# Attention steps behind a gate taken in pairs, in a kernel of banded attention followed by a mixture of experts

## Chip, cores and metric

One core of a Trainium2 chip runs the whole program. The metric is the device time of one execution in microseconds (us). The kernel before took 825.73 to 827.17 us in three runs, 827.11 us in the median.

## What is computed

Eight heads of attention, four with a plain causal window of 32 positions and four with a window of 32 positions at a distance of 4, and then four experts on its output, each weighed by a probability:

```python
mask_plain = (rel >= 0) & (rel < window)                      # window 32
mask_dil = (rel >= 0) & (rel < window * dilation) & (rel % dilation == 0)
scores = np.where(masks, scale * np.matmul(q, k.transpose(0, 1, 3, 2)), -1e9)
attn = np.exp(scores - np.max(scores, axis=-1, keepdims=True))
attn = attn / (np.sum(attn, axis=-1, keepdims=True) + 1e-09)
x = np.matmul(attn, v)                # 4 x 8 x 576 x 64, then 2304 x 512
for e in range(E):                    # 4 experts, hidden size 1024
    h = np.maximum(x @ w1[e], 0.0)
    out += p[:, e:e + 1] * (h @ w2[e])
```

## The kernel before, in words

Every large product runs as three products of rounded halves (high by high, low by high, high by low), so each operand x, w1, w2 and h is split into a high half (ScalarE, L130 or L449) and a low half (VectorE or GpSimd, L127 and L455).

**The experts' stream** is a generator, `experts`, that hands out pieces. A visit is one quarter of one expert on 768 tokens, and has 13 pieces. `mm1_b` (L475 on) has five, each a product of six TensorE matmuls of 384 columns: S2 (then ScalarE copies the bank to u2, L482), S1 (copied to s5, L487), S3 (VectorE adds the bank to s5, L491), S4 (VectorE adds to u2, L496) and A22. A22 writes into the bank that L491 reads, so TensorE can't begin it before L491 is done. `mm1_a` has two such pieces for the next visit; after the second VectorE adds (L472), ScalarE makes a hidden half (L449) and VectorE the other (L455). `mm2` has six pieces in two lots of three; a piece is one tile of 128 tokens, six matmuls of 512 columns into one of two banks, and VectorE adds the bank to the sum (L544, named acc). A tile can begin only when the tile two before it has been added. The two lots stand on the two sides of `mm1_a`'s second piece. A piece says "room" after S2, S1 and `mm1_a`'s first, and "full" after S4 and A22. VectorE, ScalarE and GpSimd work through their instructions in the order in which the program writes them.

**Attention** has 24 steps of two groups each. A step is: 24 small matmuls for the scores (`s_qk`, tile sc, 48 records in the trace), six masked maxima on VectorE (`s_max`), a subtraction on GpSimd (`s_sub`), the exponential on ScalarE (`s_exp`), the sums and reciprocals on VectorE (`s_sum`, tiles su and rc), a multiplication on GpSimd (`s_norm`), three transposes on TensorE and one copy on ScalarE (`s_tr`, tiles pt and pts), and 24 small matmuls with v (`s_av`, tile po, 48 records) with two copies to x on ScalarE. The four banks of `pa` hold sc, pt and po in turn.

**The order.** A loop over rounds n writes, at the start of a round, the parts of attention that are due (the tables `first`, `apart`, `then`), and then takes pieces of the experts' stream, with one step of the queue of splits (`step`) after each. Steps 0 to 9 are needed before the gate OPEN, which lies at 56 us. The 14 steps behind it (10 to 23) follow table `then`: one step begins in each round of PACE = 10 pieces, and the parts of four steps that are under way stand together at the round's start: `s_sub`, `s_sum`, `s_tr`, `s_av`, `s_qk`, `s_norm`, `s_exp`, `s_max`. Splits of x for later tokens (`x_part`, on VectorE for odd parts, tiles xl) are taken at pieces that say "room"; differences of x (`x_sums`, L227) run on VectorE.

Of the kernel before, what the change touches and what calls it, by code (L numbers as in the profile page):

```python
# [48 lines left out]
def kernel(  # L49
# [194 lines left out]
    def attention(ap, xrp, pa):  # L244
# [125 lines left out]
        def s_av(n, gs):  # L370
# [3 lines left out]
            for i in range(GS):  # L374
                for half in range(2):
                    for k in range(len(gs)):
                        rows = slice(KB * k, KB * (k + 1))
                        for j in range(2):
                            c = i * 128 + 64 * (j ^ k) + QB * half
                            o = i * SB + QB * half  # L380
                            nc.tensor.matmul(  # L381
                                po[k][64 * j:64 * j + 64, o:o + QB],
                                v_s[rows, j, 2 * i + half, :], ts_[rows, c:c + QB],
                                start=True, stop=True,
                            )

            for k, (b, p, gi) in enumerate(gs):
                x = x_raw(b)[:, p, :]
                src = po[k][:, :GW]
                if p < NP // 2:  # L390
                    nt = GW // DILATION
                    dst = x.rearrange("q (r t) -> q r t", r=DILATION)
                    dst = dst[:, :, gi * nt:(gi + 1) * nt]
                    src = src.rearrange("q (t r) -> q r t", r=DILATION)
                else:
                    dst = x[:, gi * GW:(gi + 1) * GW]
                if 0 < n < 3:
                    nc.vector.tensor_copy(out=dst, in_=src)
                else:
                    nc.scalar.activation(out=dst, in_=src, func=AF.Copy)  # L400

        def load_masks():
# [21 lines left out]
        return chunk, load_masks, load_qk, load_v, stages  # L424
# [234 lines left out]
    with tc.manual_schedule():  # L659
# [14 lines left out]
        pools["chunk"], load_masks, load_qk, load_v, stages = attention(ap, xr_pool, pa)  # L674
# [16 lines left out]
        steps = [rest[i:i + 2] for i in range(0, len(rest), 2)]  # L691
# [17 lines left out]
        step_at = {at(n): n for n in range(len(steps))}  # L709
# [81 lines left out]
        for n, i, names in (  # L791
# [9 lines left out]
        qk_done = av_done = 0  # L801
# [6 lines left out]
        ready["qk"] = lambda m: m < qk_done + QKB and n >= waits.get(min(m, needed[1] + 2), 0)  # L808
        fenced = {2: (3, 0), 3: (3, 1), 4: (3, 1), 7: (START + 4, 0), 8: (START + 5, 0)}
        ready["v"] = lambda m: (  # L810
            m < av_done + VB
            and (m <= needed[1] or m <= qk_done and n >= OPEN)
# [37 lines left out]

        dummies(512, 512, 128)
        ffn = experts(begin)
        for n in range(at(len(steps) - 1) + 5):
# [12 lines left out]
            for k, order in enumerate((stages[early_order], stages[2])):  # L866
                for stage, after in order:
                    m = step_at.get(n - after, -1)
                    if m >= 0 and k == (m > needed[1]):
# [11 lines left out]
                        av_done += stage == s_av  # L881
# [3 lines left out]
            if n in step_at:  # L885
                qk_done += 1
            for i, names in when.get(n, ()):
                for name in names:
                    of = first_x if i < 2 else later
                    if name is None or name == "T2":  # L890
                        prepare(x_sums, i, of=of)
                    if name is not None:
                        prepare(x_part, i, name.upper(), of=of)
# [31 lines left out]
            for piece in range(PACE if n in step_at else 4):  # L925
                full = next(ffn)
                if n == OPEN and not piece:
                    s_max(step_at[n], steps[step_at[n]])
                step()
                if full != "full":  # L930
# [4 lines left out]
                    elif full == "room":  # L935
                        step(later)
        gate.add("over")
# [61 lines left out]
```

## Time and profile before

| | |
|---|---|
| median of three runs | 827.11 us (825.73 to 827.17) |
| profiled execution | 828.18 us, its span 826.4 us |
| TensorE (PE) busy | 817.3 us, 99% of the span |
| VectorE (DVE) busy | 488.2 us, 59% |
| GpSimd (POOL) busy | 387.5 us, 47% |
| ScalarE (ACT) busy | 316.3 us, 38% |
| granted clock of TensorE | 0.994 of full speed over the span |
| chain that ended last | PE 94%, DVE 3%, ACT 1%, DMA 1% |

A busy TensorE says little here, since the ends of matmuls are modelled and overlap: the time is read from the distance between the starts of matmuls that follow each other. In the stream a matmul of 512 columns starts 0.23 us after the one before and one of 384 columns 0.17 us after.

### The profile page before, as it was taken

To read this page: it belongs to the slowest core of one execution; us is meant where nothing else is said; L and a number is where in the kernel's file an instruction comes from. 1 tells how busy PE (TensorE), PEld (TensorE's weight loads), DVE (VectorE), ACT (ScalarE), POOL (GpSimd) and SP (SyncE) were. 2 spreads that over 40 slices of the span, in tenths; PEclk is the share of its full clock that TensorE was granted. 3 is DMA by queue.
4 is the path that set the end of the run, shared out by engine and by line. 5 is a ranking of instruction groups with operands and counts; after the bars stand their busy time and mean duration, and the time that the engine had idled before them with its cause. 6 is when DMAs were issued, how large, how long until landed. Compare 5 with 4: busy or idle time off the path is not lost.

```text
span 826.4 us, 15443 instructions
## 1 busy us (share of the span) xinstructions
PE 817.3 (99%) x6162; PEld 726.3 (88%) x6162; DVE 488.2 (59%) x1058; ACT 316.3 (38%) x749; POOL 387.5 (47%) x465
## 2 busy tenths in 40 slices
PE   8999999999999999999999999999999999999998
PEld 5878888889888888989989989989989989988987
DVE  5677666675666588554554554555555555555555
ACT  2445444455545455323323323323333333333321
POOL 4436877787767689343143143143143153153110
PEclk9899999999999999999999999999999999999999
DMA  7755433434321113110010010010010010010003
GB/s 231 227 147 147 148 113 92 141 107 127 104 90 52 52 69 129 59 52 25 26 52 27 26 52 26 26 52 26 27 51 26 26 52 26 27 51 1 1 26 127
DMA packets 46770, 59.15 MB, mean 72 GB/s; under 512 B 2905, under 2 KB 36313, under 8 KB 46699
## 3 DMA queue, kind: packets, MB, share of 16 engines
q1 hardware_dynamic: 46283, 57.75, 22.4%
q8 instruction: 48, 0.79, 0.4%
q10 hardware_dynamic: 416, 0.43, 0.1%
q14 instruction: 23, 0.19, 0.1%
HBM read 53.45 MB, written 4.72 MB: 70 GB/s over the span
## 4 chain that ended last, share of the span: by engine, by line
PE 94%; DVE 3%; ACT 1%; DMA 1%; issue 1%; POOL 0%; POOLq 0%; DVEq 0%; ACTq 0%
PE m L535 47%; PE m1y L431 24%; PE m1x L431 17%; PE po L381 2%; PE sc L300 1%; PE wt L775 1%; PE pt L361 1%; DMA r<-w 1%; DVE xr L227 1%; DVE acc L544 0%; ACT hh L449 0%; DVE s L491 0%; DVE sm L314 0%; DVE hl L455 0%; ACT xh_B L130 0%
## 5 line engine op out<-in xcount | busy, mean ns | idle before, releaser
L544 DVE SCALAR_TENSOR_TENSOR acc<-m,pn,acc 128x512 f32<-128x512 f32 (+1 forms) x271 | 202.3, 747 | 129.7 <-PE m L535 129.7
L535 PE MATMUL m<-w2h,hh 128*128 128x512 f32 x578 | 227.2, 393 | 0.0
L535 PE MATMUL m<-w2l,hh 128*128 128x512 f32 x578 | 225.5, 390 | 0.0
L127 POOL TENSOR_TENSOR g2l<-r,g2h 128x256 fp32r<-128x256 f32 x116 | 85.9, 768 | 234.4 <-PE m L535 212.8
L535 PE MATMUL m<-w2h,hl 128*128 128x512 f32 x578 | 178.8, 390 | 0.3 <-DVE hl L455 0.3
L449 ACT ACTIVATE hh<-s 128x384 fp32r<-128x384 f32 x92 | 48.4, 526 | 236.7 <-DVE s L472 187.4
L535 PEld LDWEIGHTS m<-w2h,hl 128*128 128x128 f32 x578 | 108.3, 188 | 24.3 <-DVE hl L455 0.8
L535 PEld LDWEIGHTS m<-w2h,hh 128*128 128x128 f32 x578 | 108.5, 188 | 21.4 <-DVE acc L544 1.5
L535 PEld LDWEIGHTS m<-w2l,hh 128*128 128x128 f32 x578 | 108.6, 188 | 19.6
L127 POOL TENSOR_TENSOR g1l<-r,g1h 128x256 fp32r<-128x256 f32 x93 | 69.1, 763 | 69.0 <-ACT g1h L130 69.0
L127 POOL TENSOR_TENSOR w2l<-r,w2h 128x512 fp32r<-128x512 f32 x58 | 74.8, 1307 | 46.8 <-ACT w2h L130 46.6
L491 DVE TENSOR_TENSOR s<-m1y,s 128x384 f32<-128x384 f32 x46 | 25.6, 557 | 96.0 <-PE m1y L431 92.9
L482 ACT ACTIVATE u<-m1y 128x384 f32<-128x384 f32 x46 | 22.6, 492 | 146.1 <-PE m1y L431 146.1
L455 DVE SCALAR_TENSOR_TENSOR hl<-s,hh 128x384 fp32r<-128x384 f32 x92 | 56.5, 614 | 27.4 <-ACT hh L449 27.2
L431 PE MATMUL m1y<-xh_T,g2h 128*128 128x384 f32 x152 | 51.4, 338 | 0.0
L431 PE MATMUL m1y<-xl_T,g2h 128*128 128x384 f32 x152 | 51.1, 336 | 0.0
L431 PE MATMUL m1y<-xh_T,g2l 128*128 128x384 f32 x152 | 51.0, 335 | 0.0
L130 ACT ACTIVATE g2h<-r 128x256 fp32r<-128x256 f32 x120 | 41.7, 405 | 0.4 <-POOL r L168 0.4
L431 PE MATMUL m1x<-xh_B,g2h 128*128 128x384 f32 x124 | 41.6, 336 | 0.2 <-ACT s L487 0.2
L431 PE MATMUL m1x<-xl_B,g2h 128*128 128x384 f32 x124 | 41.6, 336 | 0.0
L431 PE MATMUL m1x<-xh_B,g2l 128*128 128x384 f32 x124 | 41.4, 334 | 0.0
L130 ACT ACTIVATE w2h<-r 128x512 fp32r<-128x512 f32 x64 | 38.2, 622 | 1.3 <-DMA r<-w 1.3
(133 smaller groups left out, 1490.7 us busy)
## 6 DMA issues: line engine op xcount, KB each, us to landing
r<-w SPq DMA_DIRECT2D x63, 512.0 KB, 3.3
v_s<-vw SPq DMA_DIRECT2D x48, 192.0 KB, 4.5
k_s<-kT SPq DMA_DIRECT2D x23, 224.0 KB, 4.4
q_s<-qT SPq DMA_DIRECT2D x24, 192.0 KB, 4.5
out<-acc SPq DMA_DIRECT2D x17, 256.0 KB, 2.0
r<-w SPq DMA_DIRECT2D x2, 256.0 KB, 4.6
out<-acc SPq DMA_DIRECT2D x2, 128.0 KB, 2.0
k_s<-kT ACTq DMA_DIRECT2D x1, 224.0 KB, 3.3
```

Of the source, the lines that this page charges most:

```text
L127: lo_eng.tensor_tensor(out=lo, in0=src, in1=hi.bitcast(F32), op=ALU.subtract)
L130: nc.scalar.activation(out=hi, in_=src, func=AF.Copy)
L227: nc.vector.tensor_tensor(out=quarter(i, d), in0=quarter(i, a), in1=quarter(i, b), op=ALU.subtract)
L300: nc.tensor.matmul(banks[swap][o:o + QB, i * KB:(i + 1) * KB], q_s[h, c0:c0 + QB], k_s[h, c0:c0 + KB], start=True, stop=True, skip_group_c ...
L381: nc.tensor.matmul(po[k][64 * j:64 * j + 64, o:o + QB], v_s[rows, j, 2 * i + half, :], ts_[rows, c:c + QB], start=True, stop=True,)
L431: nc.tensor.matmul(bank, w[:, k], x[:, k], start=(first and k == 0 and i == 0), stop=(last and k == 1 and i == 2), skip_group_check=True,)
L449: nc.scalar.activation(out=hi, in_=src, func=AF.Relu)
L455: nc.vector.scalar_tensor_tensor(out=lo, in0=src, scalar=0.0, in1=hi.bitcast(F32), op0=ALU.max, op1=ALU.subtract)
L482: nc.scalar.activation(out=u2, in_=x, func=AF.Copy)
L491: nc.vector.tensor_tensor(out=s5, in0=x, in1=s5, op=ALU.add)
L535: nc.tensor.matmul(po, h, w[:, d], start=(n == 0 and x == 0), stop=(n == 3))
L544: nc.vector.scalar_tensor_tensor(out=acc[:, d], in0=po, scalar=pn[:, tt, e:e + 1], in1=acc[:, d], op0=ALU.mult, op1=ALU.add,)
```

## The change

Steps 11 to 23 are taken in pairs, step 10 and step 23 alone. Rounds behind the gate have 20 pieces where two steps begin (`PACE * len(new)`). Table `then` keeps only the start of step 10. A new generator, `pairs_of_steps`, writes the parts: the transposes of the old pair at the round's start; after the next piece both steps' po (`s_av` with `hold`) and the first step's copies to x; after the next the second step's copies; after the next the scores of the new pair and the first step's maxima; and then one link of the chain (max, sub, exp, sum, norm) after each piece, the second step one piece behind the first. Pieces that say "full" are passed over, and nothing is written after them. The last step's po comes after 141 pieces behind the gate, where it came after 152.

```diff
-        then = (
-            (s_sub, 1), (s_sum, 2), (s_tr, 3), (s_av, 4), (s_qk, 0), (s_norm, 2), (s_exp, 1),
-            (s_max, 0),
-        )
+        then = ((s_qk, 0), (s_max, 0))
...
+        def pairs_of_steps(new, old, begun, loaded):
+
+            for m in old:
+                s_tr(m, steps[m])
+            if old:
+                yield
+                for m in old:
+                    s_av(m, steps[m], True)
+                    if m == old[0]:
+                        s_out(m, steps[m])
+                yield
+                for m in old[1:]:
+                    s_out(m, steps[m])
+                loaded(0, len(old))
+                yield
+            if new and not begun:
+                for m in new:
+                    s_qk(m, steps[m])
+                s_max(new[0], steps[new[0]])
+                yield
+            chain = (s_max, s_sub, s_exp, s_sum, s_norm)
+            for i in range(1, len(chain) + len(new) - 1):
+                for k, m in enumerate(new):
+                    if i - k < len(chain):
+                        chain[i - k](m, steps[m])
+                if not begun and i == 2:
+                    loaded(len(new), 0)
+                yield
...
         def at(n):
 
+            back = max(0, n - needed[1])
+            n -= back - back // 2 - (back > 0)
             return n + sum(gap for gap, last in zip((GAP, GAP - 1), needed) if n > last)
...
-            return 3 if n <= needed[1] else 4
+            return 3 if n <= needed[1] else 1
...
-            for piece in range(PACE if n in step_at else 4):
+            new, old = ([m for m in late if at(m) == i] for i in (n, n - 1))
+            turns = turn(new, old, n == OPEN, loaded)
+            if n > OPEN:
+                next(turns)
+            for piece in range(PACE * len(new) or PACE):
                 full = next(ffn)
                 if n == OPEN and not piece:
                     s_max(step_at[n], steps[step_at[n]])
+                elif full != "full" or n == OPEN:
+                    next(turns, 0)
                 step()
```

In the rows of order, lines of the changed file are later by 32 in the experts' part (L535 is L567, L544 is L576, L491 is L523, L455 is L487, L431 is L463), and a number behind a name only tells one tile from the next.

TensorE, kernel before: the groups of one step (pt transposes, po, sc) stand in one row of groups between two tiles m.

```order
L535 MATMUL m_2020<-w2h,hl 128x512 x2
L361 MATMUL pt<-ident,sm 128x128 x3
L381 MATMUL po<-pts,v_s 64x32 x24
L300 MATMUL sc<-k_s,q_s 32x64 x24
L535 MATMUL m_2113<-w2h,hh 128x512
```

TensorE, changed kernel, the same place one round later: two steps' transposes, then a tile, then two steps' po, then a product m1y and a tile (left out here but for their ends), then two steps' scores.

```order
L567 MATMUL m_2120<-w2h,hl 128x512 x2
L361 MATMUL pt<-ident,sm 128x128 x6
L567 MATMUL m_2142<-w2h,hh 128x512
...
L567 MATMUL m_2142<-w2h,hl 128x512 x2
L381 MATMUL po<-pts,v_s 64x32 x48
L463 MATMUL m1y<-xh_B_0_498,g1h 128x384
...
L567 MATMUL m_2226<-w2h,hl 128x512 x2
L300 MATMUL sc<-k_s,q_s 32x64 x48
L567 MATMUL m_2296<-w2h,hh 128x512
```

The three groups of a step no longer touch each other, and each holds two steps.

VectorE, kernel before, the end of one step's part and the experts' work behind it: the maxima (L314, the last one shown) come right behind the sums, and then three tiles' additions, the add of `mm1_a` (L472), its low half (L455) and the next three additions follow with nothing between them.

```order
L314 ISA sm,nm<-sc,mask 128x64
L314 ISA nm 128x1
L544 SCALAR_TENSOR_TENSOR acc_725<-m_2337,pn,acc_725 128x512
L544 SCALAR_TENSOR_TENSOR acc_725<-m_2349,pn,acc_725 128x512
L544 SCALAR_TENSOR_TENSOR acc_725<-m_2359,pn,acc_725 128x512
L472 TENSOR_TENSOR s_2324<-m1y,s_2324 128x384
L455 SCALAR_TENSOR_TENSOR hl<-s_2324,hh 128x384
L544 SCALAR_TENSOR_TENSOR acc_725<-m_2387,pn,acc_725 128x512
L544 SCALAR_TENSOR_TENSOR acc_725<-m_2397,pn,acc_725 128x512
L544 SCALAR_TENSOR_TENSOR acc_725<-m_2407,pn,acc_725 128x512
```

VectorE, changed kernel, the same place in the round (17) of steps 13 and 14.

```order
L576 SCALAR_TENSOR_TENSOR acc_725<-m_1932,pn,acc_725 128x512
L576 SCALAR_TENSOR_TENSOR acc_725<-m_1958,pn,acc_725 128x512
L341 TENSOR_REDUCE su<-sm 128x6
L342 TENSOR_TENSOR su<-su,eps 128x6
L345 RECIPROCAL rc<-su 128x6
L504 TENSOR_TENSOR s_1838<-m1y,s_1838 128x384
L487 SCALAR_TENSOR_TENSOR hl<-s_1838,hh 128x384
L341 TENSOR_REDUCE su<-sm 128x6
L342 TENSOR_TENSOR su<-su,eps 128x6
L345 RECIPROCAL rc<-su 128x6
L576 SCALAR_TENSOR_TENSOR acc_725<-m_1998,pn,acc_725 128x512
L576 SCALAR_TENSOR_TENSOR acc_725<-m_2009,pn,acc_725 128x512
```

One step's sums now stand ahead of the add of `mm1_a`, the other's between its low half and the addition of tile m_1998, for which the tile after next, m_2019, waits.

VectorE, changed kernel, round 20 (steps 19 and 20), at `mm1_b`: between the maxima and the add of S3 (L523, s_3132), for which A22 waits, stand two splits of x and one step's sums, and the other step's sums come right behind.

```order
L314 ISA nm 128x1
L127 TENSOR_TENSOR xl_B_1_1908<-xr,xh_B_1_1907 128x2x192
L341 TENSOR_REDUCE su<-sm 128x6
L342 TENSOR_TENSOR su<-su,eps 128x6
L345 RECIPROCAL rc<-su 128x6
L127 TENSOR_TENSOR xl_B_1_2045<-xr,xh_B_1_2044 128x2x192
L523 TENSOR_TENSOR s_3132<-m1y,s_3132 128x384
L341 TENSOR_REDUCE su<-sm 128x6
```

In the kernel before a step's sums stand right ahead of its round's maxima, and the splits of x come behind these.

## Rows read from the trace of the kernel before

**Rows 1.** The page, part 1: busy us (share of the span) xinstructions by engine.

```profile
PE 817.3 (99%) x6162; PEld 726.3 (88%) x6162; DVE 488.2 (59%) x1058; ACT 316.3 (38%) x749; POOL 387.5 (47%) x465
```

**Rows 2.** Timeline, one step's groups: start us, busy us, engine, line, operation, tiles, count.

```profile
108.15 0.49 PE L361 MATMUL pt<-ident,sm 128*128 128x128 f32 x3
108.57 0.90 PE L381 MATMUL po<-pts,v_s 64*64 64x32 f32 x48
109.40 0.72 PE L300 MATMUL sc<-k_s,q_s 64*32 64x64 f32 x48
110.06 0.50 PE L535 MATMUL m<-w2h,hh 128*128 128x512 f32 x1
110.39 0.39 PE L535 MATMUL m<-w2l,hh 128*128 128x512 f32 x1
```

**Rows 3.** Timeline of TensorE around transposes alone (46.61), scores alone (68.84), po alone (268.44).

```profile
45.80 0.34 PE L431 MATMUL m1y<-xh_B,g1h 128*128 128x384 f32 x1
45.97 0.34 PE L431 MATMUL m1y<-xh_B,g1l 128*128 128x384 f32 x1
...
46.61 0.52 PE L361 MATMUL pt<-ident,sm 128*128 128x128 f32 x3
46.88 0.48 PE L535 MATMUL m<-w2h,hh 128*128 128x512 f32 x1
47.20 0.39 PE L535 MATMUL m<-w2l,hh 128*128 128x512 f32 x1
47.43 0.39 PE L535 MATMUL m<-w2h,hh 128*128 128x512 f32 x1
...
68.58 0.34 PE L431 MATMUL m1x<-xl_B,g1h 128*128 128x384 f32 x1
...
69.50 0.44 PE L431 MATMUL m1y<-xh_B,g1h 128*128 128x384 f32 x1
...
268.17 0.34 PE L431 MATMUL m1x<-xl_B,g1h 128*128 128x384 f32 x1
...
269.27 0.50 PE L535 MATMUL m<-w2h,hh 128*128 128x512 f32 x1
```

**Rows 4.** Tiles po and sc, one record's duration: ns min/median/max, first and last start.

```profile
L381 PE MATMUL po<-pts,v_s x1152: 211/219/313, 12.3 to 269.1; 64*64 64x32 f32 x192
L300 PE MATMUL sc<-k_s,q_s x1152: 212/216/241, 5.1 to 238.0; 64*32 64x64 f32 x192
```

**Rows 5.** Timeline, from the end of mm1_a's second piece to the third tile behind.

```profile
89.46 0.39 PE L535 MATMUL m<-w2h,hh 128*128 128x512 f32 x1
89.72 0.56 DVE L472 TENSOR_TENSOR s<-m1y,s 128x384 f32<-128x384 f32 x1 [0.39 <-PE m1y L431]
90.87 0.56 DVE L455 SCALAR_TENSOR_TENSOR hl<-s,hh 128x384 fp32r<-128x384 f32 x1 [0.59 <-ACT hh L449]
91.35 0.74 DVE L544 SCALAR_TENSOR_TENSOR acc<-m,pn,acc 128x512 f32<-128x512 f32 x1
92.22 0.43 PE L535 MATMUL m<-w2h,hh 128*128 128x512 f32 x1
```

**Rows 6.** Timeline, mm1_b with two splits of x: end of S4, and A22's start.

```profile
226.18 0.52 ACT L130 ACTIVATE xh_B<-xr 128x384 fp32r<-128x384 f32 x1
226.74 0.78 DVE L127 TENSOR_TENSOR xl_B<-xr,xh_B 128x384 fp32r<-128x384 f32 x1 [0.32 <-ACT xh_B L130]
227.08 0.34 PE L431 MATMUL m1x<-xl_B,g2h 128*128 128x384 f32 x1
227.44 0.55 DVE L491 TENSOR_TENSOR s<-m1y,s 128x384 f32<-128x384 f32 x1
228.04 0.44 PE L431 MATMUL m1y<-xh_T,g1h 128*128 128x384 f32 x1 [0.62 <-DVE s L491]
```

**Rows 7.** Timeline of TensorE: two more places where it stood.

```profile
97.81 0.34 PE L431 MATMUL m1y<-xl_T,g2h 128*128 128x384 f32 x1
98.34 0.44 PE L431 MATMUL m1x<-xh_B,g2h 128*128 128x384 f32 x1 [0.20 <-ACT s L487]
...
236.66 0.30 PE L300 MATMUL sc<-k_s,q_s 64*32 64x64 f32 x4
...
238.15 0.50 PE L535 MATMUL m<-w2h,hh 128*128 128x512 f32 x1
```

**Rows 8.** Timeline of VectorE: one step's sums, its first and its last maximum.

```profile
109.32 0.54 DVE L341 TENSOR_REDUCE su<-sm 128x6 f32<-128x384 f32 x1
...
110.24 0.22 DVE L314 CUSTOM_DVE_ANT_0 sm<-sc,mask 128x64 f32<-128x64 f32 x1
...
110.97 0.22 DVE L314 CUSTOM_DVE_ANT_0 sm<-sc,mask 128x64 f32<-128x64 f32 x1
```

**Rows 9.** Groups by shape: xcount, busy us, mean ns, idle us before.

```profile
L227 DVE TENSOR_TENSOR xr<-xr 128x384 f32<-128x384 f32 x24 | 16.7, 695 | 0.3
```

More of the change, by code (lines that the diff above doesn't have):

```diff
@@ L239, in x_part, with attention @@
         yield
-    def attention(ap, xrp, pa):
+    def attention(ap, xrp, pa, steps):
         mask = ap.tile(list(masks.shape), F32, name="mask", bufs=1)
@@ L368, in s_tr, with s_av @@
             st[n] = ts_
-        def s_av(n, gs):
+        def s_av(n, gs, hold=False):
             ts_ = st.pop(n)
@@ L385, in s_av, with s_out @@
                             )
+            st[n] = po
+            if not hold:
+                s_out(n, gs)
+        def s_out(n, gs):
+            po = st.pop(n)
             for k, (b, p, gi) in enumerate(gs):
@@ L672 @@
         xr_pool = xrp.__enter__()
-        pools["chunk"], load_masks, load_qk, load_v, stages = attention(ap, xr_pool, pa)
+        steps = []
+        pools["chunk"], load_masks, load_qk, load_v, stages, turn = attention(
+            ap, xr_pool, pa, steps
+        )
         s_av, s_tr, s_max, s_exp = (stages[0][i][0] for i in (1, 2, 3, 7))
@@ L690 @@
         rest = first + rest
-        steps = [rest[i:i + 2] for i in range(0, len(rest), 2)]
+        steps += [rest[i:i + 2] for i in range(0, len(rest), 2)]
         def done(*gs):
@@ L701, in at @@
         def at(n):
+            back = max(0, n - needed[1])
+            n -= back - back // 2 - (back > 0)
             return n + sum(gap for gap, last in zip((GAP, GAP - 1), needed) if n > last)
         def lag(n):
-            return 3 if n <= needed[1] else 4
-        step_at = {at(n): n for n in range(len(steps))}
+            return 3 if n <= needed[1] else 1
+        step_at = {at(n): n for n in range(needed[1] + 2)}
         def begin():
@@ L800 @@
         first_x = []
-        qk_done = av_done = 0
+        qk_done, av_done = [0], [0]
         shares = []
@@ L849, in load_ready, with due_at, loaded @@
                     break
+        late = range(needed[1] + 1, len(steps))
         dummies(512, 512, 128)
         ffn = experts(begin)
-        for n in range(at(len(steps) - 1) + 5):
+        def due_at(n):
+            for i, names in when.get(n, ()):
+                for name in names:
+                    of = first_x if i < 2 else later
+                    if name is None or name == "T2":
+                        prepare(x_sums, i, of=of)
+                    if name is not None:
+                        prepare(x_part, i, name.upper(), of=of)
+        def loaded(qk, av):
+            qk_done[0] += qk
+            av_done[0] += av
+            load_ready()
+            if av:
+                due_at(n)
+        for n in range(at(len(steps) - 1) + 2):
             mid = 0
@@ L885 @@
             if n in step_at:
[L886 to L893, printed above, removed]
+                qk_done[0] += 1
+            if n <= OPEN:
+                due_at(n)
             place = 0 if n <= START or n >= OPEN else len(queue)
@@ L936 @@
                         step(later)
+            assert next(turns, 0) == 0
         gate.add("over")
```

10 lines of the change are left out of this document (5 added, 5 removed).

## Prediction

> **What bounds the kernel now.** The first part of the page comes first: TensorE (PE) 99% busy, VectorE (DVE) 59%, the rest below 50% [rows 1]. So time can only be won or lost where the starts of TensorE's matmuls lie further apart than their pace, and the share of busy time can't show it. The timeline of TensorE gives the pace: 0.23 us from one 512-column matmul to the next (47.20 to 47.43) and 0.17 for 384 columns (45.80 to 45.97) [rows 3]. A tile of six is 1.38, a product of six 1.04. I then read two things off the same timeline behind the gate: what attention's groups cost between two such matmuls, and where TensorE stood for another engine.
>
> **What a group costs.** Busy time less one record's duration is the spread of its starts: po 0.90 - 0.22 = 0.68 for 47 intervals, so 0.70 for 48; sc 0.72 - 0.22 = 0.50, so 0.51 [rows 2, 4]. From po's start to sc's is 0.83 [rows 2], so that switch costs 0.13. From sc's start to the stream is 0.66, so that exit costs 0.14 to 0.15, and the first matmul behind it is 0.10 late (110.06 to 110.39 is 0.33, not 0.23). The entry behind three transposes is 108.15 to 108.57, 0.42, of which the transposes are some 0.33. Alone, sc lies between matmuls 0.92 apart (68.58 to 69.50) and po between such 1.10 apart [rows 3]; less 0.17 of pace, plus 0.10 for the first matmul, that is 0.85 and 1.03. Transposes alone take 46.61 to 46.88, 0.27, plus 0.09 on the first matmul behind [rows 3].
>
> **The change: groups.** Steps 10 to 23 have 14 transposes, 14 po and 13 sc behind the gate's first piece. Ten of them were joined, 1.91 + 0.10 = 2.01 [rows 2]; four had transposes and po (0.33 + 1.03), three sc alone. Sum 10 x 2.01 + 4 x 1.36 + 3 x 0.85 = 28.1 us. Now there are six pairs and two single steps: transposes 14 x 0.27 + 8 x 0.09 = 4.5; po 6 x (1.03 + 0.70) + 2 x 1.03 = 12.4; sc 6 x (0.85 + 0.51) + 0.85 = 9.0; sum 25.9. The groups win **2.2**. If a switch inside a group of two steps costs as much as that from po to sc, 12 x 0.13 = 1.6 of it is gone; so the bounds are 0.6 and 2.2. I take 2.0, since the 48 records of two groups of heads run on at one pace already.
>
> On that switch the row shows 0.13 between po and sc [rows 2]. The Trainium skill, page "TensorE: Matmul & The Clock Gate", section "Part 3: Packing small matmuls — row/col tiling", says that a weight load overlaps the matmuls in flight only where its group of rows differs; by that letter the switch from one tile shape to another has no price of its own, the groups would win 1.3 less and the sum would end at about 832.6. The row speaks against it here.
>
> **The change: stalls that go.** Three waits hang on the old joint part. At 97.81 the next matmul comes 0.53 later, for a copy on ScalarE [rows 7]: 0.36 too long, with the late first matmul 0.46. At 236.66 to 238.15 sc takes 1.49 in place of 0.66 [rows 7]: 0.83. At 227.08 A22 starts 0.96 later in place of 0.17 [rows 6]: 0.79, and 0.10 more. Together **2.2**.
>
> **The change: stalls that come.** Before, a step's sums (109.32 to 110.24, 0.92) and its six maxima (0.146 apart, 0.88) ran beside the joint group's 2 us, in which the experts' stream gave VectorE nothing new [rows 2, 8]. Now each link stands alone between pieces. VectorE has spare time on average, but in two places it has next to none.
>
> First, the **third tile** behind `mm1_a`'s second piece. From 89.46 to 92.22 are 2.76, two tiles; within them VectorE's add of m1y, ScalarE's hidden half, hl (90.87) and acc (91.35, done at 92.09) follow each other, and the third tile starts 0.13 behind [rows 5]. What is put between the add and acc comes off TensorE's time one for one. In the round of steps 13 and 14 one step's sums stand ahead of that add: they wait for the addition of the tile before (0.74) and last 0.92, together 1.66, while the product lasts 1.04 and the add could start 0.06 behind it; it starts 0.6 late. The other step's sums (0.92) stand between hl and acc. 0.6 + 0.92 less the 0.13 of slack, and 0.1 for the late first matmul, is 1.45. The same place costs 0.9 for steps 17 and 18, plus 0.2 for a po that waits for pts behind five instructions on ScalarE, and 0.5 for 21 and 22, where only parts of the chain fall into it.
>
> Second, **A22**. It waits for the add of S3. From the end of S2 to A22 there are three products, 3.12; less the add itself (0.55 in rows 6) VectorE has 2.57 for what stands ahead. Steps 11 and 12: two sums, one set of maxima, a low half of w2 (taken as a split's 0.78 [rows 6]) are 3.5; the maxima begin a little early, so 0.8. Steps 15 and 16: two sums and two differences of x (0.70 each [rows 9]) are 3.23: 0.65. Steps 19 and 20: maxima, split, sums, split are 3.36, which alone would be 0.8; but two splits without anything else made A22 late by 0.79, because the second waited for its copy on ScalarE (226.18 + 0.52 [rows 6]), and now exp (no row of its own; taken as such a copy, 0.52) stands ahead of it too. Between 0.8 and 0.79 + 1.80 = 2.6 I take 1.8, nearer the upper end, as the wait for the copy can't be used for what stands behind. Two later `mm1_b` have splits with half of a chain: 0.9 and 1.2, like rows 6 and a little more.
>
> Sum: 0.8 + 1.45 + 0.65 + 1.1 + 1.8 + 0.5 + 0.9 + 1.2 = **8.4 us**. Behind the waiting add stand the additions of the next tiles, and TensorE is the one who waits; nothing else is late by it. ScalarE's and GpSimd's moved parts, and the loads of q, k and v now started one or two pieces later, lie beside TensorE with the next pair's scores 20 pieces (some 25 us) away: nothing, unless the chain is so late that the next transposes wait; each pair has ten pieces to spare there.
>
> **Sum:** 827.1 + 8.4 - 2.2 - 2.0 = 831.3 us. In the profiled execution, 828.18 with a span of 826.4, that is about 832.4; it lies 1.1 above the median, as before.
>
> **The rivals.**
> 1. *Half of it is absorbed.* The parts reach VectorE earlier than I place them, since the chain's links wait less on ScalarE than taken, and the stalls are 4 in place of 8.4: 827.1 + 4.2 - 4.2 = 827. For it: VectorE is 59% busy. Against it: rows 5 leave 0.13 whatever the average.
> 2. *The other side: VectorE keeps ahead of A22 and of the third tile.* If sums and maxima run in the time between two additions (a tile's 1.38 less acc's 0.74 leaves 0.64 each), they cost TensorE nothing, and groups and vanished stalls stay: 827.1 - 4.2 = 823, up to 825.4 with some rest. It decides at the third tile: the sums must be done before the add of `mm1_a` is ready. For it speaks that gaps of 0.64 come with each tile; against it, that a set of sums is 0.92 and that the order puts them just ahead of and behind that add. The Trainium skill, page "Perfetto Trace Analysis", section "Optimization Strategy", counts on this rival: where regimes differ in their busiest engine, interleaving them may help. What the rows show is that TensorE is the busiest in both.
> 3. *The waits chain.* Where a late sum makes GpSimd's multiplication, the transposes and po late too, each of six pairs stands another 0.5 to 1 us (236.66 shows 0.83 for one such [rows 7]): 835 to 838.
> 4. *The change doesn't do what it says.* The order shows the groups as told; no chance.
>
> **How the numbers follow.** Forecast, 828.8 to 834.5: 0.57. Rival 1, 825.5 to 828.8: 0.19, of which 0.14 lies within 0.2% (1.65 us, about what a measurement of this kernel can tell from no change). Rival 2: 0.13. Rival 3: 0.11. Faster: rival 2 with a little of rival 1, 0.15. The same: 0.17. Slower 0.68. The range leaves out the faster half of rival 2 and the slower part of rival 3: 825.0 to 835.0.
>
> **What would show it.** In the changed kernel's timeline po and sc of pairs should cost 1.73 and 1.36 on TensorE (right if their starts run on without a gap). The third tile behind `mm1_a` of steps 13 and 14 should start some 1.4 late, released by acc, and A22 in the round of steps 19 and 20 by over 1 us, released by the add of S3; VectorE's share of the chain that ended last should rise above its 3%. The prediction is wrong if these two places run at the pace, or if the pairs' groups show gaps of their own.

## The result and the profile after

The changed kernel takes 835.88 us in the median of four runs (833.86 to 838.63), the kernel before 826.73 us beside it: a ratio of 1.0115 with a 95% interval of 1.0083 to 1.0147, so it is slower by some 9 us. A second set of four runs of it gave 836.17 us (1.0107, 1.0081 to 1.0134). The direction of the forecast held, its size did not: 831.3 us was forecast, and 835.88 lies above the upper end of the range, 835.0.

The page of the changed kernel, parts 1 and 4: busy time by engine, then the chain that ended last.

```profile
PE 817.8 (98%) x6162; PEld 723.8 (87%) x6162; DVE 487.5 (58%) x1058; ACT 314.5 (38%) x749; POOL 388.8 (47%) x465
...
PE 90%; DVE 6%; ACT 2%; issue 1%; POOL 0%; DVEq 0%; ACTq 0%; POOLq 0%
```

Each engine has as many instructions as in [rows 1], and no busy time differs by more than 2.5 us. VectorE's part of the chain is 6% where it was 3%: the same instructions now stand where TensorE waits for them.

**How the traces are compared.** Before the gate TensorE's clock is granted at the lower level (1.2 GHz, 0.50) for a time that differs from trace to trace: 3.4 to 13.7 us in nine of the fourteen traces of this case, not at all in five. In the trace of the kernel before it is so from about 18 to 29 us, in that of e2_single (below) never. Two stretches of the kernel before; the columns are the stretch and its length, busy time by engine, granted clock, DMA share and GB/s.

```profile
20.00:22.00 2.00, 2.00 (x47) 1.60 (x48) 0.33 (x1) 1.68 (x4) 0.70 (x1) 0.50 0.98 297
22.00:24.00 2.00, 2.00 (x53) 1.71 (x50) 1.43 (x4) 1.56 (x6) 0.30 (x1) 0.50 1.01 318
```

The same stretches of e2_single:

```profile
20.00:22.00 2.00, 1.65 (x52) 1.37 (x53) 1.05 (x1) 2.00 (x8) 1.00 (x1) 1.00 0.96 306
22.00:24.00 2.00, 1.28 (x48) 1.24 (x48) 0.76 (x2) 0.36 (x2) 0.00 (x0) 1.00 0.88 273
```

The executions of the kernel before lie between 824.98 us (granted clock 1.00 over the span) and 830.27 us (0.992). So I compare traces from the last record of step 10's scores (55.93 us before, 54.84 us after) to the end, and sort what matmuls' starts lie apart beyond their pace: by attention's groups (with their switches and the late first matmul; the end of step 10's scores is in it), by waits (other gaps and the matmul behind them), and by gaps at the lower clock. The medians less this stretch lie between 54.9 and 58.3 us, so a comparison of medians can carry some 3 us from before the gate.

| us, from the trace | median | behind the gate | groups | waits | at half clock |
|---|---|---|---|---|---|
| before | 826.73 | 770.4 | 29.1 | 4.4 | 0 |
| changed | 835.88 | 779.9 | 27.3 | 14.1 | 1.6 |
| changed, e9_again | 836.17 | 779.3 | 27.2 | 13.6 | 1.7 |
| e1_held | 831.96 | 775.1 | 27.3 | 10.7 | 0 |
| e2_single | 832.69 | 777.7 | 31.0 | 9.8 | 0 |
| e3_no_sums | 830.01 | 771.7 | 27.4 | 7.2 | 0 |
| e4_no_eps | 830.26 | 772.7 | 27.3 | 8.3 | 0 |
| e5_tiny | 832.61 | 776.1 | 27.2 | 12.2 | 0 |
| e6_tile | 828.11 | 771.9 | 27.3 | 7.5 | 0 |
| e7_tile_room | 822.55 | 767.4 | 27.3 | 2.9 | 0 |
| e8_before_eps | 825.02 | 770.0 | 29.1 | 3.9 | 0 |
| e10_before_room | 824.53 | 769.6 | 29.1 | 3.7 | 0 |
| e11_hold_s3 | 835.26 | 778.4 | 27.3 | 14.2 | 0 |
| e12_hold_tile | 829.78 | 774.5 | 27.3 | 10.2 | 0 |

Behind the gate the change costs 779.9 - 770.4 = 9.5 us: the groups give 1.8, the waits cost 9.7 net, the clock 1.6.

**The groups** of a pair run on as forecast. TensorE's timeline of the changed kernel, po of one pair and then scores of the next (against [rows 2]); here and below, rows that lie between the ones shown are left out:

```profile
126.82 0.61 PE L567 MATMUL m<-w2h,hl 128*128 128x512 f32 x2
127.36 1.60 PE L381 MATMUL po<-pts,v_s 64*64 64x32 f32 x96
128.90 0.45 PE L463 MATMUL m1y<-xh_B,g1h 128*128 128x384 f32 x1
...
131.00 0.63 PE L567 MATMUL m<-w2h,hl 128*128 128x512 f32 x2
131.55 1.27 PE L300 MATMUL sc<-k_s,q_s 64*32 64x64 f32 x96
132.75 0.50 PE L567 MATMUL m<-w2h,hh 128*128 128x512 f32 x1
133.09 0.39 PE L567 MATMUL m<-w2l,hh 128*128 128x512 f32 x1
```

Two steps' po take 1.54 us from its start to the next matmul, two steps' scores 1.20; with entry and the late first matmul 1.73 and 1.40, where 1.73 and 1.36 were forecast. There is no second switch inside.

**The third tile** of the round of steps 13 and 14 (against [rows 5]); brackets give idle time and who ended it:

```profile
109.42 0.75 DVE L576 SCALAR_TENSOR_TENSOR acc<-m,pn,acc 128x512 f32<-128x512 f32 x1 [0.47 <-PE m L567]
110.08 0.54 DVE L341 TENSOR_REDUCE su<-sm 128x6 f32<-128x384 f32 x1
110.10 0.34 PE L463 MATMUL m1y<-xl_B,g1h 128*128 128x384 f32 x1
110.66 0.57 DVE L342 TENSOR_TENSOR su<-su,eps 128x6 f32<-128x6 f32 x1
...
111.37 0.52 DVE L504 TENSOR_TENSOR s<-m1y,s 128x384 f32<-128x384 f32 x1
...
112.59 0.61 PE L567 MATMUL m<-w2h,hl 128*128 128x512 f32 x2
112.96 0.55 DVE L341 TENSOR_REDUCE su<-sm 128x6 f32<-128x384 f32 x1
113.54 0.17 DVE L342 TENSOR_TENSOR su<-su,eps 128x6 f32<-128x6 f32 x1
...
113.92 1.37 DVE L576 SCALAR_TENSOR_TENSOR acc<-m,pn,acc 128x512 f32<-128x512 f32 x2
114.68 0.50 PE L567 MATMUL m<-w2h,hh 128*128 128x512 f32 x1 [1.48 <-DVE acc L576]
```

The product ends at about 110.4, but its add (L504) starts at 111.37, behind the first sums; the second sums stand between the low half and the addition, as the order said. The last matmul of x2 starts 0.23 behind 112.59, at 112.82, and the tile at 114.68 instead of 113.04: 1.64 late. The first sums last 1.3 us, because the small addition of 1e-9 (L342) takes 0.57 us here and 0.17 in the second.

**A22 and what stands behind it**, steps 19 and 20, VectorE and then GpSimd and TensorE:

```profile
197.12 0.48 DVE L342 TENSOR_TENSOR su<-su,eps 128x6 f32<-128x6 f32 x1
197.63 0.19 DVE L345 RECIPROCAL rc<-su 128x6 f32<-128x6 f32 x1
197.74 0.52 DVE L127 TENSOR_TENSOR xl_B<-xr,xh_B 128x384 fp32r<-128x384 f32 x1
198.18 0.55 DVE L523 TENSOR_TENSOR s<-m1y,s 128x384 f32<-128x384 f32 x1
198.64 0.54 DVE L341 TENSOR_REDUCE su<-sm 128x6 f32<-128x384 f32 x1
199.22 0.45 DVE L342 TENSOR_TENSOR su<-su,eps 128x6 f32<-128x6 f32 x1
...
199.88 0.52 DVE L528 TENSOR_TENSOR u<-m1x,u 128x384 f32<-128x384 f32 x1
...
196.84 0.74 POOL L127 TENSOR_TENSOR g1l<-r,g1h 128x256 fp32r<-128x256 f32 x1 [0.63 <-ACT g1h L130]
...
198.91 0.73 POOL L164 TENSOR_TENSOR r<-r 128x256 f32<-128x256 f32 x1
...
198.78 0.44 PE L463 MATMUL m1y<-xh_T,g1h 128*128 128x384 f32 x1 [1.36 <-DVE s L523]
...
200.45 0.45 PE L463 MATMUL m1x<-xh_B,g1h 128*128 128x384 f32 x1 [0.35 <-DVE u L528]
```

A22 starts 1.53 late (198.78; the matmul before it started at 197.08). Then comes a wait that the forecast did not have: the second sums stand ahead of the add of S4 (L528), and `mm1_a`'s first product waits for that, 0.51 late at 200.45. Both L342 end when a GpSimd instruction ends: 197.60 and 197.58, 199.67 and 199.64.

**A wait that stayed.** In the stream, which has the same 3762 matmuls of products and tiles in the same order in both kernels, the A22 of [rows 6] is this one of the changed kernel:

```profile
235.93 1.11 DVE L127 TENSOR_TENSOR xl_T<-xr,xh_T 128x384 fp32r<-128x384 f32 x1 [0.60 <-ACT xh_T L130]
236.39 0.34 PE L463 MATMUL m1x<-xl_B,g2h 128*128 128x384 f32 x1
236.96 0.54 DVE L523 TENSOR_TENSOR s<-m1y,s 128x384 f32<-128x384 f32 x1
237.56 0.44 PE L463 MATMUL m1y<-xh_T,g1h 128*128 128x384 f32 x1 [0.83 <-DVE s L523]
```

It was 0.79 late and is 0.99 late, again behind a split of x that waits for its copy on ScalarE.

### The profile page after: what moved, and what is told of

The parts are those of the page before. It is cut to its first block, busy times and chain, and to the rows that moved or that the text cites. A ratio compares the mean times of both kernels' runs of the same rounds, so it can differ in the third digit from the quotient of the medians.

```text
span 834.8 us, 15443 instructions
## 1 busy us (share of the span) xinstructions
PE 817.8 (98%) x6162; PEld 723.8 (87%) x6162; DVE 487.5 (58%) x1058; ACT 314.5 (38%) x749; POOL 388.8 (47%) x465
## 4 chain that ended last, share of the span: by engine, by line
PE 90%; DVE 6%; ACT 2%; issue 1%; POOL 0%; DVEq 0%; ACTq 0%; POOLq 0%
PE m L567 45%; PE m1y L463 22%; PE m1x L463 17%; PE po L381 2%; PE sc L300 2%; DVE acc L576 1%; PE wt L812 1%; DVE xr L227 1%; PE pt L361 1%; DVE su L341 1%; DVE su L342 1%; DVE sm L314 0%; DVE hl L487 0%; ACT hh L481 0%; DVE s L523 0%
## 5 line engine op out<-in xcount | busy, mean ns | idle before, releaser
L576 DVE SCALAR_TENSOR_TENSOR acc<-m,pn,acc 128x512 f32<-128x512 f32 (+1 forms) x271 | 201.9, 746 | 138.0 <-PE m L567 138.0
L567 PE MATMUL m<-w2h,hh 128*128 128x512 f32 x578 | 228.6, 396 | 2.6 <-DVE acc L576 2.6
L567 PE MATMUL m<-w2l,hh 128*128 128x512 f32 x578 | 226.0, 391 | 0.0
L567 PE MATMUL m<-w2h,hl 128*128 128x512 f32 x578 | 179.0, 390 | 0.3 <-DVE hl L487 0.3
L567 PEld LDWEIGHTS m<-w2h,hh 128*128 128x128 f32 x578 | 108.7, 188 | 25.2 <-DVE acc L576 4.7
L567 PEld LDWEIGHTS m<-w2h,hl 128*128 128x128 f32 x578 | 108.6, 188 | 24.5 <-DVE hl L487 0.8
L567 PEld LDWEIGHTS m<-w2l,hh 128*128 128x128 f32 x578 | 108.9, 188 | 19.4
L523 DVE TENSOR_TENSOR s<-m1y,s 128x384 f32<-128x384 f32 x46 | 25.5, 555 | 97.3 <-PE m1y L463 92.4
L487 DVE SCALAR_TENSOR_TENSOR hl<-s,hh 128x384 fp32r<-128x384 f32 x92 | 55.1, 599 | 27.7 <-ACT hh L481 27.2
L463 PE MATMUL m1y<-xh_T,g2h 128*128 128x384 f32 x152 | 51.4, 338 | 0.0
L463 PE MATMUL m1y<-xl_T,g2h 128*128 128x384 f32 x152 | 51.2, 337 | 0.0
L463 PE MATMUL m1y<-xh_T,g2l 128*128 128x384 f32 x152 | 51.0, 336 | 0.0
L463 PE MATMUL m1x<-xh_B,g2h 128*128 128x384 f32 x124 | 41.7, 337 | 0.1
L463 PE MATMUL m1x<-xl_B,g2h 128*128 128x384 f32 x124 | 41.7, 336 | 0.0
L463 PE MATMUL m1x<-xh_B,g2l 128*128 128x384 f32 x124 | 41.4, 334 | 0.0
```

The costliest lines, as they stand in the source:

```text
L463: nc.tensor.matmul(bank, w[:, k], x[:, k], start=(first and k == 0 and i == 0), stop=(last and k == 1 and i == 2), skip_group_check=True,)
L487: nc.vector.scalar_tensor_tensor(out=lo, in0=src, scalar=0.0, in1=hi.bitcast(F32), op0=ALU.max, op1=ALU.subtract)
L523: nc.vector.tensor_tensor(out=s5, in0=x, in1=s5, op=ALU.add)
L567: nc.tensor.matmul(po, h, w[:, d], start=(n == 0 and x == 0), stop=(n == 3))
L576: nc.vector.scalar_tensor_tensor(out=acc[:, d], in0=po, scalar=pn[:, tt, e:e + 1], in1=acc[:, d], op0=ALU.mult, op1=ALU.add,)
```

## Experiments

All are edits of the changed kernel unless said otherwise. "Behind the gate" is the stretch of the table.

**e1_held.** The generator says whether its next part holds maxima or sums, and the loop passes such parts over behind the pieces in HELD.

```diff
-                yield
+                on = [chain[i + 1 - k] for k in range(len(new)) if i + 1 - k < len(chain)]
+                yield "DVE" if s_max in on or s_sum in on else "any"
...
-                    next(turns, 0)
+                    if wants != "DVE" or (full + "_b" if full == "room" and at_b else full) not in HELD or n == OPEN:
+                        wants = next(turns, 0)
...
+        HELD = ("room_b", "S3", "t2", "t3", "a2")
```

(`room_b` is S2 and S1 of `mm1_b`, `t2` and `t3` are tiles of the first lot, `a2` is `mm1_a`'s second piece.)

> The changed kernel, but a part with VectorE work (maxima or sums) is not written after the two first pieces of mm1_b, its third, the second and third tile of the first lot, or mm1_a's second piece; it waits for the next piece. TensorE's groups of two steps stay. Theory (the loss is VectorE's sums and maxima standing ahead of the adds that TensorE waits for): the 11.8 us of new waits in the changed kernel's trace shrink to about 2 (a few splits stay ahead of A22), the 1.6 us at half clock behind them go with them, and the groups' 1.9 us and the 2.2 us of vanished waits are left: 824 to 826 us, below the kernel before. Rival (taking steps in pairs is itself what costs, through banks, copies and longer groups): 833 to 836 as in the changed kernel.

Measured 831.96 us (1.0064, 1.0039 to 1.0089). Of the 9.5 us behind the gate 4.8 are gone, 1.6 of them the clock's: more than the rival allows and less than the theory wanted. Some waits have moved: a split of x that comes with sums behind `mm1_a`'s first piece makes two third tiles late, by 0.73 and 0.71, and in two places the links are done too late for the transposes.

TensorE's timeline of this kernel at the transposes of the second pair:

```profile
96.18 0.49 PE L361 MATMUL pt<-ident,sm 128*128 128x128 f32 x3
97.29 0.55 PE L361 MATMUL pt<-ident,sm 128*128 128x128 f32 x3 [0.62 <-POOL sm L350]
97.59 0.42 PE L464 MATMUL m1x<-xh_T,g2h 128*128 128x384 f32 x1
```

The second step's transposes wait for GpSimd's multiplication: the first starts 0.89 us behind the one before it, where 0.11 is the pace. So to hold VectorE's parts back at all of these places is no remedy here.

**e2_single.** Steps begin singly, every 10 pieces; the spread stays.

```diff
-            back = max(0, n - needed[1])
-            n -= back - back // 2 - (back > 0)
```

> The spread alone: one step per round of 10 pieces, its transposes, po, scores and links each after a piece of their own, nothing in pairs. Theory (the spread of VectorE's work costs, the pairing gains): waits like the changed kernel's, some 8 to 13 us, and no gain from groups but a loss of about 2.5 us (14 x 0.36 + 14 x 1.03 + 13 x 0.85 = 30.5 against 28.1 before): 834 to 841 us. Rival (pairing costs): near the kernel before, 826 to 830 us.

Measured 832.69 us (1.0082, 1.0067 to 1.0097), below the 834 to 841 expected; behind the gate 777.7. The groups cost 31.0 in place of 29.1, 1.9 us (2.4 expected), and the waits 9.8, near the lower end of the 8 to 13 expected. The rival falls: the spread alone, without any pairs, makes the kernel slower, and 1.9 + 9.8 - 4.4 = 7.3 us is the whole of its loss. Its waits are partly others, though: five times 0.4 to 1.1 us of them stand ahead of transposes, which wait for late links.

**e3_no_sums.** No sums and reciprocals for steps 11 to 23; a constant stands in their place.

```diff
+            if n > 10:
+                st[n] = (sm, fix)
+                return
```

> The changed kernel without the sums and reciprocals of steps 11 to 23 (the products are scaled by a constant in their place), so VectorE has 13 x 1.2 us less to do and everything else stands as in the changed kernel. Theory: the late third tiles (1.75, 1.2), the late u adds (0.62, 0.63) and most of the late A22 (1.2, 1.0, part of 2.0) go, some 7 of 11.8 us, and the half clock with them: 827 to 829 us. Rival (pairing costs, or the splits and maxima alone): less than 3 us, 833 us or more.

Measured 830.01 us (1.0035, 1.0017 to 1.0052); behind the gate 771.7, 8.2 us less than the changed kernel, or 6.6 without its half clock. The third tiles of steps 13/14 and 17/18 and the adds of S4 are on time, as the theory said; the three A22 behind splits of x stay late (1.26, 0.95, 1.20), where the changed kernel has 1.53, 0.99 and 1.20. So the sums have next to nothing to do with the last two. The median is 1 to 3 us above what was expected; it is the one with the most time before the gate (58.3 us, granted clock 0.992 to 0.999 over the span).

**e4_no_eps.** The same without the addition of 1e-9.

```diff
-            nc.vector.tensor_tensor(
-                out=su, in0=su, in1=eps.to_broadcast([128, 2 * GS]), op=ALU.add
-            )
```

> The changed kernel without the addition of 1e-9 to the sums (L342, one instruction of 128x6 per step, 0.17 to 0.64 us in the trace). Theory (a set of sums costs 1.2 us and not the 0.92 that the prediction took, because this small addition takes 0.47 in the median): about nine sets of sums stand on TensorE's path, 9 x 0.4 = 3 to 4 us less than the changed kernel: 831 to 833 us. Rival (its length is waiting that the next instruction then takes over): no change, 835 to 836 us.

Measured 830.26 us (1.0046, 1.0022 to 1.0070); behind the gate 772.7, which is 7.2 us less than the changed kernel, or 5.6 without its half clock, where 3 to 4 were expected. The smallest instruction of the chain costs more than half of what the change loses.

**e5_tiny.** In place of that addition, an instruction of the same size that reads one operand.

```diff
-            nc.vector.tensor_tensor(
-                out=su, in0=su, in1=eps.to_broadcast([128, 2 * GS]), op=ALU.add
-            )
+            nc.vector.reduce_sum(out=su, in_=su.unsqueeze(2), axis=mybir.AxisListType.X)
```

> The changed kernel with the addition of 1e-9 replaced by another instruction of the same size on VectorE, a reduction of 128x6 over a length of one, which reads one operand (the addition itself is left out). It tells an instruction more from a wait: in the changed kernel's trace the addition L342 lasts 0.17 us or until 0.02 us after the end of the GpSimd instruction under way, 0.48 in the median. Theory (an operation of two operands in the memory that GpSimd reads waits for it): the small reduction lasts some 0.1 to 0.2 us every time, and the stretch behind the gate falls from 779.9 us to some 774, near the 772.7 without the instruction; about 831 us in the median. Rival (any instruction between the sums and the reciprocals costs that): 835 to 836 us and 0.4 to 0.5 us for one.

Measured 832.61 us (1.0072, 1.0045 to 1.0099); behind the gate 776.1, of which 0.83 is a wait inside one group of scores that the other traces don't have. Here is the instruction in line 342 (count; shortest, median and longest in ns; first and last start), first in the kernel before, behind the gate:

```profile
L342 DVE TENSOR_TENSOR su<-su,eps x14: 166/370/792, 84.5 to 258.4; 128x6 f32<-128x6 f32 x14
```

The changed kernel, the same:

```profile
L342 DVE TENSOR_TENSOR su<-su,eps x14: 165/477/641, 61.7 to 258.3; 128x6 f32<-128x6 f32 x14
```

And e5_tiny over its whole span:

```profile
L342 DVE TENSOR_REDUCE su<-su x24: 159/159/164, 9.6 to 257.8; 128x6 f32<-128x6 f32 x24
```

With one operand it lasts 0.16 us each time, though 22 of the 24 overlap a GpSimd instruction. So the length of the addition is a wait for GpSimd, and that is shown. What it is worth lies between the 2.2 us that are less behind the gate (778.3 without half clock, 776.1) and 3.0 (without the wait in the scores); the other 2.6 to 3.4 of the 5.6 us go with the instruction itself, which makes a set 0.19 us longer than in e4_no_eps from its start to that of the next instruction; how much of it each place passes on to TensorE is not shown. The 774 us expected put too much on the wait.

**e6_tile.** As e4_no_eps, and parts with VectorE work passed over behind tiles 2 and 3 and `mm1_a`'s second piece only (the edit of e1_held with HELD = `("t2", "t3", "a2")`).

> The changed kernel without the addition of 1e-9 (the sums are at least 1, so it changes no bit), and no part with VectorE work is written behind the second and third tile of the first lot and behind mm1_a's second piece. Theory (what stands ahead of mm1_a's add or between its low half and the next addition comes off TensorE one for one): the three late third tiles left without the addition (0.84, 0.59, 0.33, and 0.1 each for the first matmul) go: the stretch behind the gate 772.7 - 2.0 = 770.7 us, 828 us in the median. Rival (the parts then collide somewhere else, as sums behind mm1_a's first piece did with a split of x): 772 to 774 us, 830 to 831 in the median.

Measured 828.11 us (1.0004, 0.9984 to 1.0025): no different from before. Behind the gate 771.9. The third tiles are on time, all three; a wait of 0.54 inside one group of scores is new, so 771.9 lies between theory and rival. What is left are the three late A22 (1.26, 0.90, 1.20) and a copy.

**e7_tile_room.** In addition splits of x are taken behind the last two tiles of the second lot, not behind S2 and S1.

```diff
-        nc.scalar.activation(out=u2, in_=x, func=AF.Copy)
-        yield "room"
+        nc.scalar.activation(out=u2, in_=x, func=AF.Copy)
+        yield "b"
...
-                    elif full == "room":
+                    elif full in ("room", "t5", "t6"):
```

> As the run before in this set, and in addition the splits of x are not taken behind the two first pieces of mm1_b but behind the two last tiles of the second lot. Theory (three late A22 of 0.9 to 1.3 us each, and 0.23 for a late copy, come from splits whose copies ScalarE makes too late): the stretch behind the gate another 3.5 us shorter, 767 us, 824 us in the median, 2 below the kernel before. Rival (the splits collide with the additions there, or are wanted earlier): 770 to 773 us.

Measured 822.55 us (0.9958, 0.9935 to 0.9980): faster than the kernel before by 3.5 us, and 13 below the changed one. Behind the gate 767.4. The timeline of the place where A22 was 1.53 late:

```profile
188.66 0.19 DVE L342 RECIPROCAL rc<-su 128x6 f32<-128x6 f32 x1
189.22 0.56 DVE L521 TENSOR_TENSOR s<-m1y,s 128x384 f32<-128x384 f32 x1 [0.37 <-PE m1y L461]
189.81 0.34 PE L461 MATMUL m1x<-xl_B,g2h 128*128 128x384 f32 x1
189.99 0.34 PE L461 MATMUL m1y<-xh_T,g1h 128*128 128x384 f32 x1
```

The add (L521 here) waits for TensorE now, not TensorE for it, and A22 follows at the pace (189.81 to 189.99).

**e8_before_eps.** The kernel before without the addition.

> The kernel before without the addition of 1e-9. Theory (its sums stand beside the joint group on TensorE, so their length hardly counts there): the stretch behind the gate 770.4 us becomes 769.5 to 770.4, 825.5 to 826.5 us in the median. Rival (the addition costs TensorE time wherever it stands): 3 us less, 823 us.

Measured 825.02 us (0.9991, 0.9973 to 1.0010); behind the gate 0.5 us less than before. The rival falls: in the kernel before, where a step's sums run beside the joint group, the same instruction costs nearly nothing, although there too L342 is long (up to 0.79).

**e9_again.** The changed kernel once more.

> The changed kernel once more, unchanged. What is asked is whether the 1.6 us at half clock behind the waits of 195.7 to 200.5 us belong to the change. If those waits bring TensorE's clock down, it is at 1.2 GHz for some 3 us behind them again, and the stretch behind the gate takes 779.9 us again; if the fall was chance, the waits are the same to 0.1 us and the stretch takes 778.0 to 778.3. In either case 833 to 838 us in the median.

Measured 836.17 us; behind the gate 779.3. All waits are the same to 0.03 us, and the clock falls behind the same ones. Stretches of the changed kernel behind the waits of steps 19 and 20 (columns as above, the granted clock third from the end):

```profile
198.50:200.50 2.00, 1.37 (x7) 1.05 (x7) 1.86 (x6) 0.60 (x2) 1.87 (x3) 1.00 0.02 8
200.50:204.00 3.50, 3.50 (x11) 3.11 (x12) 2.27 (x4) 2.34 (x6) 2.74 (x4) 0.56 0.00 0
```

The same of e9_again:

```profile
197.50:199.50 2.00, 1.36 (x7) 1.04 (x7) 1.86 (x6) 0.59 (x2) 1.88 (x3) 1.00 0.07 22
199.50:203.00 3.50, 3.50 (x10) 3.20 (x11) 2.12 (x4) 2.16 (x6) 2.72 (x3) 0.53 0.00 0
```

And of e12_hold_tile:

```profile
193.50:195.80 2.30, 1.32 (x6) 1.00 (x6) 2.16 (x6) 0.53 (x1) 2.22 (x3) 1.00 0.14 48
195.80:199.30 3.50, 3.28 (x16) 2.88 (x17) 2.90 (x6) 2.75 (x6) 3.30 (x5) 1.00 0.00 0
```

Twice TensorE runs at half clock for some 3 us behind the waits, and the 1.6 us belong to the change in both of its traces. But e12_hold_tile has the same three waits (0.23, 1.53, 0.52) and keeps its clock. That the waits alone bring the clock down is therefore not shown, and what else is needed stays open.

**e10_before_room.** The kernel before, without the addition and with the splits of e7_tile_room.

> The kernel before, without the addition of 1e-9 and with the splits of x moved as in the run with 822.55 us, but with single steps and joint parts: against that run it tells what taking steps in pairs is worth once the waits are gone. Theory (the pairs' groups save 1.8 us of switches; moved splits save the one late A22 of 0.8): the stretch behind the gate 770.0 - 0.9 = 769 us against 767.4 there, 824 us in the median. Rival (all of that run's gain is from the splits and the addition): 767.4 us or less, 822.5 us or less.

Measured 824.53 us (0.9979, 0.9961 to 0.9996); behind the gate 769.6 (769 expected) against 767.4 with pairs: 1.8 of the difference are groups (29.1 and 27.3), the rest waits. So pairs are worth some 2 us once little else is in the way; that rests on one trace of each, since the intervals of the two medians (824.53 and 822.55) overlap.

**e11_hold_s3.** The edit of e1_held with HELD = `("S3",)`; the addition stays.

> The changed kernel, except that no part with VectorE work is written behind the third piece of mm1_b (S3), so no sums stand between its add and the add of S4. Theory (at two places in the changed kernel the sums there made the add of S4, and with it mm1_a's first product, late by 0.51 and 0.52, and 0.11 for the first matmul): both go, 1.25 us less, 776.8 us behind the gate apart from a fallen clock (778.0 there); the third tiles and A22 stay late. Rival (those two waits are the splits' doing): no change.

Measured 835.26 us (1.0095, 1.0071 to 1.0120); behind the gate 778.4. Both late adds of S4 are gone, but 1.25 us are not won: A22 of steps 19 and 20 is 2.06 late in place of 1.53, as its second split lasts 1.05 us, not 0.52, beside GpSimd, and the last transposes wait 1.1 us for the sums that were held back. Only the half clock is less. What was held back came back at other places, which the expectation left out.

**e12_hold_tile.** The same with HELD = `("t2", "t3", "a2")`; the addition stays.

> The changed kernel, except that no part with VectorE work is written behind the second and third tile of the first lot and behind mm1_a's second piece; the addition of 1e-9 stays. Theory: the three late third tiles (1.64, 1.09, 0.32, and 0.11 each for the first matmul) go, 3.4 us less: 774.6 us behind the gate apart from a fallen clock; the parts move by a piece or two, so an A22 may become up to 0.5 later. Rival (the late third tiles come from the long groups of two steps ahead of them): they stay, 778 us.

Measured 829.78 us (1.0047, 1.0025 to 1.0069); behind the gate 774.5, 3.8 us less than the changed kernel without its half clock (778.3), where 3.4 were expected. The third tile of steps 13 and 14, 1.64 late in the changed kernel, in this one (L508 is the add of `mm1_a`):

```profile
108.81 0.56 DVE L508 TENSOR_TENSOR s<-m1y,s 128x384 f32<-128x384 f32 x1 [0.38 <-PE m1y L464]
...
110.85 0.61 PE L573 MATMUL m<-w2h,hl 128*128 128x512 f32 x2
111.31 0.43 PE L573 MATMUL m<-w2h,hh 128*128 128x512 f32 x1
```

The add waits for TensorE, and the tile starts at the pace (111.08 and 0.23). The other two third tiles are on time too. Beyond what was expected, A22 of steps 11 and 12 is on time (1.2 us), and a third tile in the round of steps 11 and 12 is 0.46 late in its place. The groups of two steps are all still there; the scores of steps 11 and 12 and of 21 and 22 come three pieces later. The third tile's waits are shown to be what stood between `mm1_a` and the next addition.

## Why the prediction was right in its direction and wrong in its size

**Groups: right.** 2.0 us forecast, 1.8 in the trace and 1.8 again between e10_before_room and e7_tile_room. The Trainium skill's rule on row groups (page "TensorE: Matmul & The Clock Gate", section "Part 3: Packing small matmuls — row/col tiling"), read as a free switch, would have left 0.7; the trace has 1.8, so the switch has its price here. The rule is on weight loads and says nothing of a change of tile shape, so the trace speaks only against that reading of it.

**Stalls that go: two of three.** 2.2 us forecast. The two places of [rows 7] no longer wait. The A22 of [rows 6], 0.89 of the 2.2, does: it is 0.99 late at 237.56, for the old cause. The forecast took it as gone and put 0.9 and 1.2 on two later `mm1_b`, of which this is one, so the sum came out nearly the same by luck: 0.89 less and 1.10 more, where one stall grew by 0.2.

**Stalls that come: mostly the right places, mis-sized.** This is the term that failed: 8.4 us forecast, 11.7 in the trace. (The clock's 1.6 us come on top.)

| place | forecast | measured |
|---|---|---|
| A22, steps 11/12 | 0.8 | 1.20 |
| third tile, 13/14 | 1.45 | 1.75 |
| A22, 15/16 | 0.65 | 1.05 |
| third tile and po, 17/18 | 1.1 | 1.35 |
| S4 and A22, 19/20 | 1.8 | 1.98 |
| third tile, 21/22 | 0.5 | 0.43 |
| two later A22 | 2.1 | 2.41 |
| add of S4, twice | none | 1.25 |
| third tile, step 10 | none | 0.31 |

Two steps of the working failed. The price of a set of sums was taken from one row group, [rows 8], as 0.92 us; there L342 lasted 0.17, which is the shortest of its 14 behind the gate. Their median was 0.37, in the changed kernel 0.48, so a set is 1.2 us. That accounts for 1.0 to 1.8 us of the 1.8 by which the first seven rows were too small, as e5_tiny shows: a set is 0.9 us again there, and the seven rows add up to 8.4 us, or to 9.2 with the wait of 0.8 inside the scores of steps 11 and 12, behind which A22 of these steps falls to 0.2. The row of the two later A22 has no part in this: they are late behind splits with or without the sums (e3_no_sums). What brought a split ahead of the second of them, which was on time before, is not shown: the exponential that now stands between ScalarE's copies, or the queue of splits, which the change fills behind po and no longer at the round's start. And the sentence "nothing else is late by it" was wrong: the sums that the order shows right behind the add of S3 stand ahead of the add of S4, and `mm1_a`'s first product waits for that one. The row was in front of me, and only its first waiter was followed: 1.25 us, twice an add of S4.

**The clock: not in the sum.** 1.6 us, in both traces of the changed kernel; what it takes beside the waits stays open (e9_again).

So the miss adds up behind the gate: 4.2 us were forecast (8.4 - 2.2 - 2.0) and 9.5 measured. Of the 5.3 between them 3.3 are the stalls that come, 1.6 the clock and 0.2 the groups; the rest lies in small differences.

**The rivals.** Half absorbed, and VectorE keeping ahead: both fell in the first order of the parts. The Trainium skill's page "Perfetto Trace Analysis", section "Optimization Strategy", says that interleaving may help: here VectorE is 58% busy, and TensorE waits at a dozen places; e7_tile_room, at other places, is 3.5 us below the kernel before. The rival of chained waits named the right time (835 to 838) for a wrong reason: in the changed kernel no transposes wait for late links, only one po, for 0.15 us. It is in e1_held, e2_single and e11_hold_s3 that links come late.

**Profiled execution.** It was forecast 4.2 us above that of before and came 8.4 above (834.8 and 826.4 of span): 9.5 behind the gate, less 1.1 before it, where this execution was at the lower clock for less time.

## What to carry to other kernels

Before work of an engine with time to spare is spread over a stream, list for each place the instruction ahead of which it lands and everyone who waits for that; here the new waits were 11.7 us in the parts' first order, and at the places of e7_tile_room, without the small addition, two of 0.3 us and a few smaller ones. Take the price of an instruction from its shortest, median and longest over the stretch, not from one place, above all for a small one beside a second engine on the same memory. The pairing that saved 2 us of switches was worth them only once the waits it made were gone.

## What the runs showed of the hardware that was not expected

Operations of VectorE with two operands in SBUF, the memory that GpSimd works in too, waited for the GpSimd instruction under way: the addition of 128x6 lasted 0.17 us alone, or where GpSimd's instruction ended within its first 0.14 us, and otherwise ended 0.02 to 0.03 us behind GpSimd's instruction, up to 0.79 us; the reduction of the same size, with one operand, lasted 0.16 us in 24 of 24. In these traces it goes by the place of the operands: behind the gate of the changed kernel the low half (L487) lasted up to 1.13 us where both its operands lie in SBUF (138 times, 30 of them begun with a GpSimd instruction under way) and at most 0.56 us where one lies in a bank of TensorE's results (48 times, 28 so begun). The Trainium skill, page "SBUF — State Buffer", section "Who interferes with whom", says so: a VectorE instruction with two SBUF inputs contends with a GpSimd instruction that reads SBUF, and `tensor_reduce` never does. The traces agree on both: the sums (L341, a reduction) lasted 0.51 to 0.55 us in all 14 of the changed kernel behind the gate. The splits of x, also of two operands, go the same way: 0.52 us at 197.74 in the changed kernel and 1.05 at the same place in e11_hold_s3, where a GpSimd instruction was under way for its first 0.6 us.
